# Bringing the second q chunk early, one context step further forward, in a fused attention and FFN kernel

## The chip, the cores and the metric

The program runs on one core of a Trainium2 chip. The runs were spread over several chips, and every experiment had the kernel before timed beside it on its own chip. The metric is device time of one execution in microseconds (us), as the median of several runs.

PE is the matmul engine, DVE the vector engine, ACT the scalar engine; SP issues the DMA transfers told here. PSUM is the memory that matmuls write to.

## The reference

Layer norm of x (2048 x 640), then 32 heads of attention over the last 512 keys (head size 192), a SwiGLU feed-forward net on the same normed input, and out = x + attention * silu(ffn):

```python
xn = layernorm(x)
q = (xn @ wq)                              # 2048 x (32*192)
scores = q @ k[-512:].T * 192**-0.5        # per head
o = softmax(scores) @ v[-512:]
s = o @ wo
g = silu((silu(xn @ w_gate) * (xn @ w_up)) @ w_down)
return x + s * g
```

## The kernel before

Two heads make a pair (16 pairs). For each pair there are four steps, one for each block of 512 queries. A pair first runs its four *score steps*: for each of four key chunks a product (a score tile of 128 x 1024 in fp32) and an exp of it on ACT. In between stand the three q chunks of the step that follows. Then it runs its four *context steps*: P times V, the division by the row sums, a DMA transpose of the result, and, woven in, the product with wo (the *wo tiles*) for the step two earlier. Steps are numbered through: pair 0 has 0 to 3, pair 1 has 4 to 7.

PSUM holds two buffers called `sc` (scores, wo tiles, some context accumulators) and two called `mm` (q chunks, context accumulators). A buffer can be written again when the engine that reads it has finished.

```python
def q_rows(i, j, between=None):            # chunk j of step i's q
    pr, b = divmod(i, NB)
    if j == 0:
        qTs[i] = qpool.tile([P, 3, 512], bf, name="qT")
    q_ps = mm_tile()
    for c in range(NC):                    # NC = 5
        if c == NC - 1 and between:
            between()                      # drops the held wo half here
        for h, r in enumerate((lo, hi)):
            nc.tensor.matmul(...)          # 10 in all, 64 rows each
    nc.vector.reduce_sum(qTs[i][:, j, :], ...)   # DVE, frees q_ps

def scores(i, kc):
    sc = ... sc_tile()
    for j in range(3): ...                 # 6 matmuls
    nc.scalar.activation(p_t[:, :, :], sc[:, :, :], ACT.Exp, scale=scale)

def divide(i, q2, acc, alone):             # alone: steps 0 and 1, and some of the last pair
    nc.vector.reciprocal(r[:], a_v[:, :, :, Dh : Dh + 1])
    for k in range(2):
        if k == 0 and alone:
            nc.vector.tensor_tensor(O_b[...], a_k[...], r[...], ALU.mult)
            continue
        for h in range(2):
            nc.scalar.activation(O_b[...], a_k[...], ACT.Copy, scale=r[...])
    nc.sync.dma_start_transpose(out=OT_b[...], in_=O_b[...])

def woven(i):                              # a context step with wo tiles of step i-2
    (a, b), (w, x, y, z) = (pv(i, 0), pv(i, 1)), (wo_tile(i - 2, qt) for qt in range(4))
    for part in (*a[:2], drop, w[0], *b[:2], w[1], x[0], *a[2:], x[1], y[0], *b[2:], y[1], z[0]):
        part()
    held.append(z[1])                      # the last wo half waits for the next drop

# ... second half of a wo tile ends with the DVE copy of sc into sacc (pair 0)
# or the DVE add to sacc (later pairs)

EARLY = (NB + 1, 0)                        # step 5, chunk 0
for pr in range(NPAIR):
    for b in range(NB):                    # score steps
        i = pr * NB + b
        for kc in range(KC):
            if kc < 3 and i + 1 < NS and (i + 1, kc) != EARLY:
                q_rows(i + 1, kc, drop)
            scores(i, kc)
            # ...
    for b in range(NB):                    # context steps
        i = pr * NB + b
        if i < 2:
            two(pv(i, 0), pv(i, 1))        # no wo tiles yet
            if i == 1:
                q_rows(*EARLY)             # the early chunk
        elif pr < last - 1:
            woven(i)
        # ...
```

The softmax here doesn't subtract the row's maximum and nothing guards it: scores larger than these inputs give would overflow.

Of the kernel before, what the change touches and what calls it, by code (L numbers as in the profile page):

```python
# [15 lines left out]
def kernel(  # L16
# [28 lines left out]
    NB = Sq // 512  # L45
# [28 lines left out]
    def mm_tile():  # L74
        return psum.tile([P, 2, 512], f32, name="mm", tag="mm")
# [40 lines left out]
    def load_v(pr):  # L116
        for h in range(2):
            nc.sync.dma_start(
                out=V_p[:, :, h, 0:Dh],
                in_=vv[2 * pr + h, k0:Sk, :].rearrange("(p j) d -> p j d", j=KC),  # L120
            )

    def load_wo(pr):
        wo_p = pairs[pr]["wo"] = wpool.tile([P, 3, D], bf, name="wo_p")
        nc.sync.dma_start(
            out=wo_p[:], in_=wo[pr * PD : (pr + 1) * PD, :].rearrange("(j p) d -> p j d", p=P)
        )
# [4 lines left out]
    def transpose_k(pr, j):  # L132
        d = pairs[pr]
        if j == 0:
            d["KT"] = kpool.tile([P, 3, W], bf, name="KT")
            d["ssum"] = kpool.tile([P, 3], f32, name="ssum")
            d["nmean"] = kpool.tile([P, 3], f32, name="nmean")
        nc.sync.dma_start_transpose(
            out=d["KT"][:, 0:3, j * P : (j + 1) * P],
            in_=d["K"][:, j, :, :].rearrange("p h d -> p (h d)"),  # L140
        )

    def sum_k(pr, c):
        d = pairs[pr]
        nc.vector.reduce_sum(d["ssum"][:, c : c + 1], d["KT"][:, c, :], axis=AX.X)
# [6 lines left out]
    def centre_k(pr, c):  # L152
        d = pairs[pr]
        if c == 0:
            d["khat"] = kpool.tile([P, 3, W], bf, name="khat", bufs=2)
            nc.vector.tensor_scalar(d["nmean"][:], d["ssum"][:], -1.0 / W, None, op0=ALU.mult)
        s, dst, ch, src = CENTRE[c]
        nc.vector.tensor_scalar(
            d["khat"][dst, s, :], d["KT"][src, ch, :], d["nmean"][src, ch : ch + 1], None, op0=ALU.add
        )  # L160

    qTs = {}
# [257 lines left out]

    def q_rows(i, j, between=None):
        pr, b = divmod(i, NB)
        if j == 0:
            qTs[i] = qpool.tile([P, 3, 512], bf, name="qT")
        q_ps = mm_tile()
        for c in range(NC):
            if c == NC - 1 and between:
                between()
            for h, r in enumerate((lo, hi)):
                nc.tensor.matmul(  # L430
                    q_ps[:, h, :], pairs[pr]["wq"][r, c, j * P : (j + 1) * P], xnT[r, c, b * 512 : (b + 1) * 512],
                    start=(c == 0), stop=(c == NC - 1),
                )
        with nc.allow_low_precision(reason="a sum of two, rounded once, like a copy out of PSUM"):
            nc.vector.reduce_sum(  # L435
                qTs[i][:, j, :], q_ps[:, :, :].rearrange("p h n -> p n h"), axis=AX.X
            )

    def scores(i, kc):
        khat, qT, ks = pairs[i // NB]["khat"], qTs[i], slice(kc * P, (kc + 1) * P)  # L440
        sc = mm_tile() if i == NS - 1 and kc < 2 else sc_tile()
        for j in range(3):
            for h, r in enumerate((lo, hi)):
                nc.tensor.matmul(  # L444
                    sc[:, h, :], khat[r, j, ks], qT[r, j, :], start=(j == 0), stop=(j == 2)
                )
        p_t = ppool.tile([P, 2, 512], bf, name="p_t")
        nc.scalar.activation(p_t[:, :, :], sc[:, :, :], ACT.Exp, scale=scale)  # L448
        Ps.setdefault(i, {})[kc] = p_t

    def pv(i, q2):

        pr, b = divmod(i, NB)
        st = {}

        def part(p):
            if p == 0:
                if q2 == 0:
                    Obs[i] = opool.tile([P, 4, 2, Dh], bf, name="O_b")
                    tag = "OT_l" if late(i) and pr < last else "OT_b"  # L460
                    OTs[i] = otpool.tile([P, 12, P], bf, name=tag, tag=tag, bufs=2 if tag == "OT_l" else 3)
                st["alone"] = i < 2 or (pr == last and 2 * b + q2 < 5)
                st["acc"] = sc_tile() if st["alone"] and q2 and b < 2 else mm_tile()
            acc = st["acc"]
            turn, h = divmod(p, 2)
            for kc in range(KC):
                for n, r in enumerate((lo, hi)):
                    k = n ^ turn
                    qt = 2 * q2 + k
                    m = nc.tensor.matmul(  # L470
                        acc[:, k, h * 256 : h * 256 + Dh + 1],
                        Ps[i][kc][r, h, qt * P : (qt + 1) * P], V_p[r, kc, h, 0 : Dh + 1],
                        start=(p == 0 and kc == 0), stop=(turn == 1 and kc == KC - 1),
                        skip_group_check=True,
                    )
                    after(m, st)
            if p == 1:
                turned(m, st)
            if p == 3:
                divide(i, q2, acc, st["alone"])  # L480

        return [lambda p=p: part(p) for p in range(4)]
# [46 lines left out]
    def load_xr(t):  # L529
        xrs[t] = finp.tile([P, D], bf, name="x_r", bufs=8)  # L530
        nc.sync.dma_start(out=xrs[t][:], in_=x2[t * P : (t + 1) * P, :])
# [66 lines left out]
    def wo_full(i, qt):  # L598
        pr, b = divmod(i, NB)
        t = 4 * b + qt  # L600
        sc = sc_tile()
        for n in range(2):
            wo_mm(sc[:, n, 0:HD], i, qt, n)
        s_t = sacc[:, t, :].rearrange("p (n d) -> p n d", n=2)
        if pr == 0:
            nc.vector.tensor_copy(out=s_t, in_=sc[:, :, 0:HD])
        else:
            nc.vector.tensor_tensor(s_t, s_t, sc[:, :, 0:HD], ALU.add)

        if pr == last - 1 or late(i + NB):  # L610
            nc.gpsimd.tensor_tensor(sacc[:, t, :], sacc[:, t, :], g2[:, t, :], ALU.mult)
            if pr < last - 1:
                add_x(t)

    def add_x(t):
        nc.gpsimd.tensor_tensor(sacc[:, t, :], sacc[:, t, :], xrs[t][:], ALU.add)
# [32 lines left out]
            nc.sync.dma_start(out=out2[t * P : (t + 1) * P, :], in_=ob[:])  # L649

    held = []
    EARLY = (NB + 1, 0)

    def two(x, y):
        for part in (*x[:2], *y[:2], *x[2:], *y[2:]):
            part()
# [5 lines left out]
    def woven(i):  # L662
# [5 lines that stand above are left out]
        held.append(z[1])  # L668

    for pr in range(NPAIR):  # L670
        for b in range(NB):
# [5 lines that stand above are left out]
                if pr < last:  # L677
                    if b == 0:
                        transpose_k(pr + 1, kc)
                    elif b == 2 and kc < 3:  # L680
                        sum_k(pr + 1, kc)
                    elif b == 3:
                        centre_k(pr + 1, kc)
                        if kc == 3:
                            centre_k(pr + 1, 4)
            if b == 0:
                load_v(pr)
                if pr >= last - 1:
                    for t in range(8):
                        load_xr(t + 8 if pr < last else t)  # L690
                        if pr == last:
                            add_x(t)
        if pr == last:
            break
        for b in range(NB):
            i = pr * NB + b
            if i < 2:
                two(pv(i, 0), pv(i, 1))
                if i == 1:
                    q_rows(*EARLY)  # L700
            elif pr < last - 1:
                woven(i)
            else:
                for q2 in range(2):
                    pv_full(i, q2)
                    wo_full(i - 2, 2 * q2)
                    wo_full(i - 2, 2 * q2 + 1)
            if b == 0 and pr + 2 < NPAIR:
                load_k(pr + 2)
            elif b == 1 and pr + 2 < NPAIR:  # L710
                load_wq(pr + 2)
            elif b == 2:
                load_wo(pr + 1)
    i = last * NB
# [43 lines left out]
```

## Time and profile before

| | before |
|---|---|
| time | 925.96 us (925.85 to 926.03, 3 runs) |
| span of the profiled run | 924.2 us |
| PE, DVE, ACT busy | 99%, 62%, 51% |
| recorded waits of PE from 168 to 888 us | one, 0.5 us |

How to read it: PE is the bound, so only its stops count. The recorded idle time of PE runs from the modelled end of a matmul to the next start, so it understates a stop; the starts of successive groups, compared with the same group where nothing waits, give its full length.

### The profile page before, as it was taken

How to read it: one execution, taken by the hardware profiler on the slowest of the kernel's cores; microseconds unless marked ns; L12 is line 12 of the kernel's file. 1: busy time of each engine (PE TensorE's matmuls, PEld its weight loads, DVE VectorE, ACT ScalarE, POOL GpSimd, SP SyncE). 2: the span in 40 equal slices, each digit the busy share in tenths (PEclk: the TensorE clock that was granted, in tenths of full speed). 3: DMA queues.
4: the chain of work that ended last, by engine and by line, in shares of the span. 5: the costliest groups of instructions: out<-in, count | busy, mean ns of one | idle time of the engine just before them, and what ended most of it. 6: DMA issues, size and time to landing. Idle time of an engine off the chain costs nothing.

```text
span 924.2 us, 25783 instructions
## 1 busy us (share of the span) xinstructions
PE 916.6 (99%) x11101; PEld 622.6 (67%) x11101; DVE 576.1 (62%) x844; ACT 473.8 (51%) x847; POOL 100.1 (11%) x387
## 2 busy tenths in 40 slices
PE   9999999999999999999999999999999999999997
PEld 5455555575858585868686767676767777776665
DVE  6433331467676767676666667676767676767655
ACT  4222223546464656555556465655555555656561
POOL 0000000000000000000000000000000000002977
PEclk9999999999999999999999999999999999999999
DMA  9321510044544443444636252635371717162624
GB/s 297 74 54 35 114 35 1 1 81 86 83 83 80 86 80 86 72 94 66 100 59 107 57 109 53 112 50 116 45 121 40 126 37 129 35 132 74 145 47 140
DMA packets 243810, 77.18 MB, mean 84 GB/s; under 512 B 224624, under 2 KB 243696, under 8 KB 243696
## 3 DMA queue, kind: packets, MB, share of 16 engines
q1 hardware_dynamic: 242640, 74.72, 40.7%
q8 instruction: 87, 1.43, 0.7%
q10 hardware_dynamic: 1056, 0.82, 0.3%
q14 instruction: 27, 0.22, 0.1%
HBM read 39.45 MB, written 2.62 MB: 46 GB/s over the span
## 4 chain that ended last, share of the span: by engine, by line
PE 98%; DMA 1%; DVE 1%; ACTq 0%; issue 0%; ACT 0%; DVEq 0%
PE mm L430 22%; PE sc L565 19%; PE sc L444 18%; PE mm L470 16%; PE sc L276 11%; PE mm L298 6%; PE sc L539 3%; PE mm L522 2%; PE mm L539 1%; DMA wu_sb<-in_B_w_up_dram 1%; PE mm L276 0%; PE mm L311 0%; PE sc L522 0%; PE sc L470 0%; PE mm L444 0%
## 5 line engine op out<-in xcount | busy, mean ns | idle before, releaser
L448 ACT ACTIVATE p_t<-sc 128x1024 bf16<-128x1024 f32 x254 | 253.0, 1022 | 128.9 <-PE sc L444 128.9
L435 DVE TENSOR_REDUCE qT<-mm 128x512 bf16<-128x1024 f32 x189 | 230.9, 1223 | 91.6 <-PE mm L430 89.2
L500 ACT ACTIVATE O_b<-mm,r 128x192 bf16<-128x192 f32 x486 | 164.6, 421 | 183.6 <-issue 162.4
L430 PE MATMUL mm<-xnT,wq_p 64*128 64x512 bf16 x1890 | 240.0, 376 | 0.0
L590 DVE TENSOR_TENSOR sacc<-sacc,sc 128x640 f32<-128x640 f32 x200 | 164.2, 821 | 89.5 <-PE sc L565 89.5
L565 PE MATMUL sc<-wo_p,OT_b 64*128 64x320 bf16 x2592 | 217.0, 296 | 0.0
L444 PE MATMUL sc<-qT,khat 64*128 64x512 bf16 x1524 | 198.1, 376 | 0.5 <-DVE sacc L588 0.5
L470 PE MATMUL mm<-V_p,p_t 64*128 64x193 bf16 x3520 | 186.2, 242 | 0.1
L470 PEld LDWEIGHTS <-p_t 64*128 64x128 bf16 x3584 | 162.4, 93 | 12.9 <-issue 0.6
L430 PEld LDWEIGHTS <-wq_p 64*128 64x128 bf16 x1890 | 104.7, 94 | 95.7 <-issue 0.5
L565 PEld LDWEIGHTS <-OT_b 64*128 64x128 bf16 x2592 | 139.4, 94 | 22.2
L444 PEld LDWEIGHTS <-khat 64*128 64x128 bf16 x1536 | 85.1, 94 | 80.1 <-issue 0.7
L553 POOL MEMSET turn_t<- 128x1 f32 x328 | 32.2, 98 | 697.0 <-PE mm L470 474.6
L284 DVE TENSOR_TENSOR hT<-sc,sg 128x512 bf16<-128x512 f32 x46 | 31.7, 690 | 85.2 <-ACT sg L283 85.1
L283 ACT ACTIVATE sg<-sc 128x512 bf16<-128x512 f32 x46 | 27.3, 596 | 72.4 <-PE sc L276 72.4
L276 PE MATMUL sc<-xnT,wu_sb 128*128 128x512 bf16 (+1 forms) x260 | 59.1, 354 | 0.2 <-DMA wu_sb<-in_B_w_up_dram 0.2
L276 PE MATMUL sc<-xnT,wg_sb 128*128 128x512 bf16 (+1 forms) x260 | 59.2, 354 | 0.1
L298 PE MATMUL mm<-wd_sb,hT 128*128 128x320 bf16 x384 | 56.6, 299 | 0.0
L489 DVE RECIPROCAL r<-mm 128x4 f32<-128x4 f32 x124 | 22.7, 183 | 47.8 <-PE mm L470 36.3
L298 PEld LDWEIGHTS <-hT 128*128 128x128 bf16 x384 | 37.6, 98 | 18.9
L276 PEld LDWEIGHTS <-wu_sb 128*128 128x128 bf16 x285 | 26.3, 98 | 27.2 <-DMA wu_sb<-in_B_w_up_dram 0.4
L276 PEld LDWEIGHTS <-wg_sb 128*128 128x128 bf16 x285 | 26.4, 98 | 23.1 <-issue 0.2
(68 smaller groups left out, 372.9 us busy)
## 6 DMA issues: line engine op xcount, KB each, us to landing
wo_p<-in_A_wo_dram SPq DMA_DIRECT2D x16, 480.0 KB, 4.2
K_p<-in_A_k_cache_dram SPq DMA_DIRECT2D x32, 192.0 KB, 3.3
V_p<-in_A_v_cache_dram SPq DMA_DIRECT2D x32, 192.0 KB, 3.1
wq_p<-in_A_wq_dram SPq DMA_DIRECT2D x64, 80.0 KB, 3.2
wq_p<-in_A_wq_dram SPq DMA_DIRECT2D x16, 160.0 KB, 3.4
x_r<-in_A_x_dram SPq DMA_DIRECT2D x16, 160.0 KB, 3.9
x_t<-in_A_x_dram SPq DMA_DIRECT2D x14, 160.0 KB, 3.0
OT_b<-O_b SPq DMA_TRANSPOSE x124, 2.8
```

Source lines behind the costliest of these rows:

```text
L276: nc.tensor.matmul(out, w_sb[:, c, f * P : (f + 1) * P], xnT[:, c, qc], start=(c == 0), stop=(c == NC - 1),)
L298: nc.tensor.matmul(dn[:, 0:HD], hTs[b][:, f, ti * P : (ti + 1) * P], wd_sb[:, f, cols], start=(f == 0), stop=(f == NF - 1),)
L430: nc.tensor.matmul(q_ps[:, h, :], pairs[pr]["wq"][r, c, j * P : (j + 1) * P], xnT[r, c, b * 512 : (b + 1) * 512], start=(c == 0), stop=(c ...
L435: nc.vector.reduce_sum(qTs[i][:, j, :], q_ps[:, :, :].rearrange("p h n -> p n h"), axis=AX.X)
L444: nc.tensor.matmul(sc[:, h, :], khat[r, j, ks], qT[r, j, :], start=(j == 0), stop=(j == 2))
L448: nc.scalar.activation(p_t[:, :, :], sc[:, :, :], ACT.Exp, scale=scale)
L470: m = nc.tensor.matmul(acc[:, k, h * 256 : h * 256 + Dh + 1], Ps[i][kc][r, h, qt * P : (qt + 1) * P], V_p[r, kc, h, 0 : Dh + 1], start=(p ...
L500: nc.scalar.activation(O_b[:, qt, h, :], a_k[:, h, 0:Dh], ACT.Copy, scale=r[:, k, h, :])
L539: nc.tensor.matmul(ps, OTs[i][:, 3 * qt + j, :], pairs[i // NB]["wo"][:, j, n * HD : (n + 1) * HD], start=(first and j == 0), stop=(end an ...
L553: st["turn"] = nc.gpsimd.memset(turn_t[:], 0.0)
L565: m = nc.tensor.matmul(ps[:, n, 0:HD], OTs[i][r, 3 * qt + j, :], pairs[i // NB]["wo"][r, j, n * HD : (n + 1) * HD], start=(turn == 0 and j ...
L590: nc.vector.tensor_tensor(s_t, s_t, sc[:, :, 0:HD], ALU.add)
```

## The change

In steps 0 and 1 there is no wo tile to put between, so one q chunk of a later step stands there as filler. The change takes another chunk (the second of step 5, not the first) and puts it one context step sooner. The intent is that step 4 again begins with a whole q chunk ahead of its first scores, as in the other pairs, and that the filler's own reduce is long done when its buffer is needed.

```diff
     def q_rows(i, j, between=None):
-        if j == 0:
+        if i not in qTs:
             qTs[i] = qpool.tile([P, 3, 512], bf, name="qT")
@@
-    EARLY = (NB + 1, 0)
+    EARLY = (NB + 1, 1)
@@
                 two(pv(i, 0), pv(i, 1))
-                if i == 1:
+                if i == 0:
                     q_rows(*EARLY)
```

## The prediction

> **What bounds the kernel now.** I read the page's parts 1 and 2 first, to see whether one engine carries the whole span, then the list of waits, to see whether that engine ever stops in the part that the change touches, and last the timelines of PE, DVE and ACT from 190 to 216 us, to get each margin in hundredths of a microsecond.
>
> ```profile
> PE 916.6 (99%) x11101; PEld 622.6 (67%) x11101; DVE 576.1 (62%) x844; ACT 473.8 (51%) x847; POOL 100.1 (11%) x387
> PEclk9999999999999999999999999999999999999999
> ```
>
> PE is busy 99% of 924.2 us at full granted clock. So every microsecond that PE stops is a microsecond of the end, and nothing else counts. The list of waits for PE between 168 and 214 us has one line, and from 214 to 888 us it is empty:
>
> ```profile
> PE sc L444 <- DVE sacc L588: 0.5, 1, 0.5
> ```
>
> So the most that the page itself offers is this wait. The PE timeline shows where it lies: at the seam between the context steps of pair 0 and the score steps of pair 1.
>
> ```profile
> 196.93 1.24 PE L430 MATMUL mm<-xnT,wq_p 64*128 64x512 bf16 x10
> 198.12 0.84 PE L470 MATMUL mm<-V_p,p_t 64*128 64x193 bf16 x16
> 198.79 0.58 PE L565 MATMUL sc<-wo_p,OT_b 64*128 64x320 bf16 x6
> 199.49 0.84 PE L470 MATMUL mm<-V_p,p_t 64*128 64x193 bf16 x16
> ...
> 209.06 0.99 PE L565 MATMUL sc<-wo_p,OT_b 64*128 64x320 bf16 x12
> 210.56 0.82 PE L444 MATMUL sc<-qT,khat 64*128 64x512 bf16 x6 [0.51 <-DVE sacc L588]
> 211.20 1.04 PE L430 MATMUL mm<-xnT,wq_p 64*128 64x512 bf16 x8
> 212.06 0.59 PE L565 MATMUL sc<-wo_p,OT_b 64*128 64x320 bf16 x6
> 212.47 0.40 PE L430 MATMUL mm<-xnT,wq_p 64*128 64x512 bf16 x2
> 212.69 0.83 PE L444 MATMUL sc<-qT,khat 64*128 64x512 bf16 x6
> 213.34 1.26 PE L430 MATMUL mm<-xnT,wq_p 64*128 64x512 bf16 x10
> ```
>
> The first line is the early q chunk (chunk 0 of step 5). Because it was brought early, the first scores of step 4 come straight after the wo half at 209.06, with nothing between. They need the score buffer of the wo tile before, which DVE still copies out. The next pair's seam is the undisturbed form, with a whole q chunk ahead of the scores and no wait:
>
> ```profile
> 255.69 0.99 PE L565 MATMUL sc<-wo_p,OT_b 64*128 64x320 bf16 x12
> 256.50 1.04 PE L430 MATMUL mm<-xnT,wq_p 64*128 64x512 bf16 x8
> 257.37 0.59 PE L565 MATMUL sc<-wo_p,OT_b 64*128 64x320 bf16 x6
> 257.77 0.40 PE L430 MATMUL mm<-xnT,wq_p 64*128 64x512 bf16 x2
> 257.99 0.83 PE L444 MATMUL sc<-qT,khat 64*128 64x512 bf16 x6
> ```
>
> Starts are the better clock. Twelve wo matmuls take 255.69 to 256.50, or 0.81, so at the first seam PE was free at 209.06 + 0.82 = 209.88, and the scores began at 210.56: the stop is 0.68 us, not 0.51. The same reading finds a second stop that the list of waits hides: six wo matmuls take 0.41 (257.37 to 257.77), yet after 198.79 the next line begins at 199.49, 0.70 later. So 0.29 us are lost there. The DVE and ACT timelines name both releasers:
>
> ```profile
> 198.22 1.22 DVE L435 TENSOR_REDUCE qT<-mm 128x512 bf16<-128x1024 f32 x1 [0.29 <-PE mm L430]
> ...
> 209.68 0.82 DVE L588 COPY sacc<-sc 128x640 f32<-128x640 f32 x1 [0.23 <-PE sc L565]
> ```
>
> ```profile
> 194.67 0.73 ACT L500 ACTIVATE O_b<-mm,r 128x192 bf16<-128x192 f32 x2 [1.58 <-DVE r L489]
> ...
> 197.34 0.73 ACT L500 ACTIVATE O_b<-mm,r 128x192 bf16<-128x192 f32 x2 [1.26 <-DVE r L489]
> ```
>
> The reduce of the early chunk ends at 199.44 and PE goes on at 199.49; the copy ends at 210.50 and PE goes on at 210.56. A release therefore takes about 0.05 us. A third, smaller stop: the early q chunk needs 1.075 us of issue (ten matmuls, 211.20 to 212.06 for eight), so PE could go on at 198.00, but went on at 198.12, just after the ACT work of 197.34 ended (198.07).
>
> **What the Trainium skill says.** "Perfetto Trace Analysis", section "Tensor Engine Instruction (MATMUL, LD_WEIGHTS)", says that a matmul's end is estimated and only its start observed. The trace agrees: consecutive groups overlap by about 0.17 us, and 0.51 recorded is 0.68 by starts. "TensorE: Matmul & The Clock Gate", section "The mechanism" in Part 3, says that matmuls keep program order while weight loads may be pulled ahead. So one blocked matmul holds all behind it, and a chunk helps only if it stands before the blocked one in the program. "TensorEngine Tiling (Array Packing)", section "Key Properties", says that a change of tiling mode drains the array. Every PE group from 168 to 216 us is 64*128, so moving a chunk among them adds no change of mode. "Perfetto Trace Analysis", section "Matmuls", asks that groups rotate over PSUM banks so that evacuation overlaps the next group; here two score and two mm buffers rotate, and the stops above are where that rotation is too short.
>
> **The change, part by part.** Nothing is added or removed. PE has the same 22,204 rows in both programs, ACT, POOL and SP keep their order, and DVE moves one reduce. Two parts:
>
> 1. The early chunk moves from after context step 1 to after step 0, so it runs at 194.26 instead of 196.93. It is followed by step 1, whose first accumulator takes the buffer that ACT frees at 194.67 + 0.73 = 195.40. PE could go on at 194.26 + 1.075 = 195.335 and goes on at about 195.45: the third stop stays as it was, 0.12. Step 1 then ends at 198.12 as before, and the context of step 2 starts at 198.12 as before. Its second accumulator no longer waits for the reduce (which now ends near 196.8) but for step 1's division. Step 1's accumulator ends 1.19 later than before, so its ACT work ends at 198.07 + 1.19 = 199.26, and PE is released at 199.31. It could have gone at 199.20. Before it went at 199.49, so this saves 0.18, not 0.29.
>
> 2. The chunk that is early is the second. The first stands again at its place, with the held wo half in it. From 209.88 - 0.18 = 209.70: eight q matmuls to 210.56, the wo half to 210.97, the last two q to 211.19, first scores at 211.19. The copy they need ended at 210.32, so the stop of 0.68 is gone. But now the second scores follow at once, with no chunk between. They would go at 211.19 + 0.65 = 211.84, and in the built program they wait for DVE (before, for ACT): they take the buffer of the held wo half. Its copy starts 0.62 after that half's start (257.37 and 257.99 in the next pair), so at 211.19, ends at 212.01, and releases at 212.07. A new stop of 0.23. The third q chunk starts at 212.07 + 0.65 = 212.72, against 213.34.
>
> Sum: -0.18 (reduce) -0.68 (copy) +0.23 (new stop) = -0.63; by the end points, 213.34 - 212.72 = 0.62. After that the programs are the same and PE never waits until 888 us, so the shift reaches the end whole: 925.96 - 0.62 = 925.34 us.
>
> Margins that I checked for a further stop. Exp of the first scores starts near 212.05 and ends near 213.08; the third scores need its buffer at 212.72 + 1.07 = 213.79. The second exp ends near 214.1 and the fourth scores come at 214.44. The reduce of the third chunk ends near 215.2, and step 5 needs its q near 216.2. The transposes of step 1's output are issued after the K loads, at 199.49 before; their operands are now ready at 199.26 and 199.94, the second issued near 201.2, so they keep their time. All hold, the closest by 0.2 us.
>
> **The rivals.** (a) The wait is only moved. If the copy of the held half came later, or the second scores also had to wait for an exp, the new stop would eat the gain: about 925.9. For it: two score steps stand back to back beside an exp of 1.02 us. Against it: back-to-back scores stand in every step (those x12 lines) without a wait. (b) The whole gain, 0.29 + 0.68 = 0.97, giving 924.99: it needs both replacement waits to be nothing. Against it: the copy lasts 0.82 and only 0.65 of scores covers most of it. (c) A loss. The later division of step 1 could delay the transposes, and the wo halves of step 3 would stop for a DMA. The profile gives a median of 2.8 us to landing, so the first lands by about 203 and the use is near 204.8. If it failed, up to 1 us: 926 to 926.4. (d) Nothing at all, because the chip varies: the three runs of before span 0.18 us, less than a third of the expected gain.
>
> **Range and chances.** The largest possible gain by the trace is about 1.1 us (0.68 + 0.29 + 0.12) and the plausible loss some tenths, both far from 2% (18.5 us). The centre is 925.34; rivals (a) and (b) lie about half a microsecond to each side, and chip to chip I allow 0.2. So 924.9 to 925.8. Faster by over 2%: 0.01; within 2%: 0.98; slower: 0.01.
>
> **What would show it.** The wait of 0.5 under the first scores of step 4 is gone. The first new chunk runs from about 194.26; the second accumulator of step 2 starts at about 199.31; first scores near 211.19 after eight q, six wo and two q matmuls; second scores near 212.07, 0.88 after the first instead of 0.65, with a small recorded idle (some 0.05) put down to the copy; third chunk near 212.72. I am wrong if the second scores start at 211.84 (rival b), if a wait for ACT or DMA shows up, or if the shift at 214 us is not the shift at the end.

## The result and the profile after

| | before | after |
|---|---|---|
| time, median | 925.85 us (925.52 to 926.03, 5 runs) | 925.04 us (924.93 to 925.59, 5 runs) |
| ratio | | 0.9993, 95% interval 0.9979 to 1.0006 |
| span of the profiled run | 924.2 us | 923.7 us |
| PE busy in it | 916.6 us (99%) | 917.0 us (99%) |

The three runs of the table before are the first three of these five. The ratio is the mean time of one kernel's runs over that of the other's in the same rounds, so it is not quite the ratio of the two medians. The verdict is "same": 0.8 us by the medians, 0.6 us by the ratio, and an interval that includes 1. This timing alone would not settle such a change; the trace does.

The list of waits for PE after the change, whole:

```profile
PE sc L219 <- DVE zero_t L173: 1.2, 1, 1.2
PE sc L276 <- DMA wu_sb<-in_B_w_up_dram: 0.5, 1, 0.5
PE mm L539 <- DVE s_f L640: 0.2, 1, 0.2
```

The 0.5 before the scores (L444) is gone. What is left lies at the very start and the very end of the kernel. The timeline of PE after the change (start, duration, line, operation, output and inputs, count):

```profile
194.44 1.24 PE L430 MATMUL mm<-xnT,wq_p 64*128 64x512 bf16 x10
195.63 0.84 PE L470 MATMUL mm<-V_p,p_t 64*128 64x193 bf16 x16
...
198.97 0.58 PE L565 MATMUL sc<-wo_p,OT_b 64*128 64x320 bf16 x6
199.50 0.84 PE L470 MATMUL mm<-V_p,p_t 64*128 64x193 bf16 x16
...
209.87 1.04 PE L430 MATMUL mm<-xnT,wq_p 64*128 64x512 bf16 x8
210.74 0.59 PE L565 MATMUL sc<-wo_p,OT_b 64*128 64x320 bf16 x6
211.14 0.40 PE L430 MATMUL mm<-xnT,wq_p 64*128 64x512 bf16 x2
211.36 1.70 PE L444 MATMUL sc<-qT,khat 64*128 64x512 bf16 x12
212.88 1.26 PE L430 MATMUL mm<-xnT,wq_p 64*128 64x512 bf16 x10
```

This run reached the first context matmul at 191.77, before it was 191.59, so 0.18 is to be taken from every time here when it is held against the prediction. The reader is to see three things. The second accumulator of step 2 follows the wo half ahead of it by 0.53 (198.97 to 199.50), where it was 0.70 in the kernel before; the reduce that it waited for then now ends at 196.95. The first scores come at once after the chunk (211.14 to 211.36). And twelve score matmuls take 1.52 to the next chunk (211.36 to 212.88), where twelve without a stop take 1.30: the new stop of 0.22 that the wait list doesn't show.

Three lines of other engines belong to these places: the reduce of the early chunk, which no longer stops PE, the ACT division of step 1's accumulator, which releases PE at the first place, and the DVE copy of the held wo half, which releases it at the last:

```profile
195.72 1.23 DVE L435 TENSOR_REDUCE qT<-mm 128x512 bf16<-128x1024 f32 x1 [0.29 <-PE mm L430]
```

```profile
198.72 0.73 ACT L500 ACTIVATE O_b<-mm,r 128x192 bf16<-128x192 f32 x2 [2.46 <-DVE r L489]
```

```profile
211.36 0.82 DVE L588 COPY sacc<-sc 128x640 f32<-128x640 f32 x1 [0.85 <-PE sc L565]
```

The division ends at 199.45 and PE goes on at 199.50. The copy ends at 212.18, and the second scores started at 212.88 - 0.65 = 212.23. (Asked for the window 212.22 to 212.40 alone, the trace gives 212.24, which is 0.88 after the first scores.)

### The profile page after: what moved, and what is told of

Same layout as the page of the kernel before. It is cut to its first block, busy times and chain, and to the rows that moved or that the text cites. A ratio compares the mean times of both kernels' runs of the same rounds, so it can differ in the third digit from the quotient of the medians.

```text
span 923.7 us, 25785 instructions
## 1 busy us (share of the span) xinstructions
PE 917.0 (99%) x11101; PEld 626.2 (68%) x11101; DVE 576.2 (62%) x844; ACT 473.7 (51%) x847; POOL 100.1 (11%) x387
## 3 DMA queue, kind: packets, MB, share of 16 engines
q8 instruction: 87, 1.43, 0.7%
## 4 chain that ended last, share of the span: by engine, by line
PE 98%; DMA 1%; DVE 0%; ACTq 0%; issue 0%; DVEq 0%
PE mm L430 22%; PE sc L565 19%; PE sc L444 18%; PE mm L470 16%; PE sc L276 11%; PE mm L298 6%; PE sc L539 3%; PE mm L522 2%; PE mm L539 1%; DMA wu_sb<-in_B_w_up_dram 1%; PE mm L276 0%; PE mm L311 0%; PE sc L522 0%; PE sc L470 0%; PE mm L444 0%
## 5 line engine op out<-in xcount | busy, mean ns | idle before, releaser
L444 PE MATMUL sc<-qT,khat 64*128 64x512 bf16 x1524 | 198.4, 377 | 0.1
L444 PEld LDWEIGHTS <-khat 64*128 64x128 bf16 x1536 | 85.9, 94 | 79.0 <-issue 0.4
L298 PE MATMUL mm<-wd_sb,hT 128*128 128x320 bf16 x384 | 56.6, 300 | 0.0
L298 PEld LDWEIGHTS <-hT 128*128 128x128 bf16 x384 | 37.5, 98 | 18.9
```

Of the source, the lines that this page charges most:

```text
L298: nc.tensor.matmul(dn[:, 0:HD], hTs[b][:, f, ti * P : (ti + 1) * P], wd_sb[:, f, cols], start=(f == 0), stop=(f == NF - 1),)
L444: nc.tensor.matmul(sc[:, h, :], khat[r, j, ks], qT[r, j, :], start=(j == 0), stop=(j == 2))
```

## The experiments

Two measures serve all of them. The **seam** is the time by starts from the first context matmul of pair 0 to the first q chunk of step 6: the stretch in which the two programs differ. The **rest** is from there to the start of the last three wo matmuls of the kernel. A seam without any stop should last 24.12 (before) - 0.68 - 0.29 - 0.12 = 23.03 us.

| kernel | seam starts | seam | rest | time, median (lowest to highest) | before, same chip |
|---|---|---|---|---|---|
| before | 191.59 | 24.12 | 703.17 | 925.85 | |
| after | 191.77 | 23.49 | 703.19 | 925.04 (924.93 to 925.59) | 925.85 |
| after, again | 191.40 | 23.48 | 703.20 | 925.17 (925.14 to 925.34) | 925.82 |
| after, third time | 191.48 | 23.49 | 703.19 | 925.25 (925.07 to 925.47) | 926.00 |
| second chunk, late place | 192.55 | 23.66 | 703.17 | 925.36 (925.07 to 926.44) | 925.82 |
| first chunk, early place | 191.79 | 23.95 | 703.19 | 925.74 (925.45 to 926.38) | 925.82 |
| no chunk early | 191.29 | 24.14 | 703.16 | 925.48 (925.36 to 925.66) | 925.82 |
| third chunk, early place | 191.37 | 23.90 | 703.19 | 925.59 (925.55 to 926.02) | 926.10 |
| wo half sooner | 191.38 | 23.28 | 703.17 | 924.96 (924.73 to 925.93) | 926.10 |
| DVE divides | 191.57 | 23.24 | 703.20 | 925.36 (924.86 to 925.44) | 926.10 |
| both mends | 191.95 | 23.03 | 703.20 | 925.17 (924.79 to 925.62) | 926.10 |
| both mends, again | 191.12 | 23.03 | 703.20 | 924.58 (924.50 to 924.65) | 926.00 |

The rest is the same to 0.04 us in all twelve profiles, so nothing that happens in the seam is given back or multiplied later. The start of the seam varies by 1.43 us between profiles. This scatter arises in the first 40 us of the program: the first product of the down projection (L298) starts between 38.92 and 40.35 us, and from there to the seam it is 152.19 to 152.20 us in all twelve. From the last three wo matmuls to the end of the span it is 5.25 to 5.34 us. So in the profiles the times differ by the first 40 us and by the seam, and by nothing else above 0.1 us. One source of the scatter is in the lists of waits: in the "second chunk, late place" run, which started its seam last, PE stood 1.2 us for the first gate weights, and in the first "both mends" run it stood 0.5 us for the up weights. The runs that were only timed have no trace; that their scatter has the same source is likely, but not shown.

### The changed kernel again

No edit. It also served as the yardstick on the same chip as the next three.

> The changed kernel once more, as the yardstick for the runs beside it. The seam is counted by starts on PE, from the first context matmul of pair 0 to the first q chunk of step 6; it was 215.71 - 191.59 = 24.12 us before and 215.26 - 191.77 = 23.49 after. Theory (three named stops, each with its releaser): 23.49 again, with stops of 0.12 (third stop, ACT division), 0.10 (second accumulator of step 2, ACT division) and 0.23 (second scores of step 4, copy of the held wo half). Rival (the 0.63 is chance of one run): a seam that differs by over 0.05. Timed: 0.4 to 0.8 us under before.

Measured: seam 23.48, and 23.49 in a third profile.

> The changed kernel a third time, beside the version with both mends on one chip. Theory: seam 23.49; timed 0.4 to 0.8 us under before.

The seam is reproducible to 0.01 us; the medians lie 0.65 and 0.75 under before on the same chips. The 0.63 of the first profile was no chance.

### Only the choice of the chunk

```diff
-    EARLY = (NB + 1, 0)
+    EARLY = (NB + 1, 1)
@@     (and "if i not in qTs"; the place stays i == 1)
```

> Only the choice of the chunk changes: the second chunk is early, but still after context step 1. Theory (the two parts add up): the stop of 0.68 before the first scores of step 4 is gone and 0.23 comes before the second scores, while the second accumulator of step 2 still waits 0.29 for the reduce: seam 24.12 - 0.45 = 23.67, second accumulator 0.70 after the wo half that precedes it. Rival (the place of the chunk makes the gain): 24.12. Timed: about 0.45 us under before, if the end follows.

Measured: seam 23.66. The timeline of this kernel:

```profile
199.75 0.58 PE L565 MATMUL sc<-wo_p,OT_b 64*128 64x320 bf16 x6
200.45 0.84 PE L470 MATMUL mm<-V_p,p_t 64*128 64x193 bf16 x16
...
212.31 1.70 PE L444 MATMUL sc<-qT,khat 64*128 64x512 bf16 x12
213.84 1.26 PE L430 MATMUL mm<-xnT,wq_p 64*128 64x512 bf16 x10
```

The 0.70 from wo half to accumulator is there as before, and the two scores take 1.53. So the choice of the chunk is worth 0.46 of the 0.63 and brings the new stop with it.

### Only the place

```diff
-                if i == 1:
+                if i == 0:
                     q_rows(*EARLY)
@@     (EARLY stays (NB + 1, 0))
```

> Only the place changes: the first chunk is early, after context step 0. Theory: the stop at the second accumulator of step 2 falls from 0.29 to 0.10 or 0.12, the stop of 0.68 before the first scores of step 4 stays: seam 24.12 - 0.18 = 23.94. Rival (the place alone makes the gain, the copy wait dissolves because everything before it is sooner): 23.5. Timed: about 0.2 us under before, inside the spread.

Measured: seam 23.95. The stop in front of the scores is untouched:

```profile
209.08 0.99 PE L565 MATMUL sc<-wo_p,OT_b 64*128 64x320 bf16 x12
210.58 0.82 PE L444 MATMUL sc<-qT,khat 64*128 64x512 bf16 x6 [0.51 <-DVE sacc L588]
```

The place is worth 0.17. The two parts add up: 0.46 + 0.17 = 0.63. The rival held that the copy's wait would dissolve once everything before it is sooner. It doesn't, because the copy moves along with the wo tile that it reads. By the timer this part is lost in the scatter (925.74 against 925.82).

### No early chunk at all

```diff
-    EARLY = (NB + 1, 1)
+    EARLY = None
@@
-                if i == 0:
-                    q_rows(*EARLY)
```

> No chunk is early: all three of step 5 stand in step 4, as in the other pairs. The same matmuls in all. Theory: the stops before the scores of step 4 (0.68, 0.23) are both gone, since a whole chunk stands ahead of each, and so is the third stop; but the context steps of step 2 come 1.2 us sooner, and its first wo half has to wait for the transpose of step 0's output (issued at 195.4, 2.8 us at least to landing): a stop of 0.6 to 1.0 put down to DMA or shown as a late weight load. Seam 23.03 + 0.6 to 1.0 = 23.6 to 24.1. Rival (an early chunk is of no use any more): seam 23.0 to 23.1, and about 1.0 us faster than before.

Measured: seam 24.14, at the upper edge and a little beyond. There were two stops, not one. The timeline:

```profile
196.63 0.83 PE L470 MATMUL mm<-V_p,p_t 64*128 64x193 bf16 x16
197.98 0.58 PE L565 MATMUL sc<-wo_p,OT_b 64*128 64x320 bf16 x6 [0.51 <-DMA OT_b<-O_b]
...
203.51 0.57 PE L565 MATMUL sc<-wo_p,OT_b 64*128 64x320 bf16 x6
204.33 0.58 PE L565 MATMUL sc<-wo_p,OT_b 64*128 64x320 bf16 x6 [0.25 <-DMA OT_b<-O_b]
```

By starts they are 197.98 - 196.63 - 0.67 = 0.68 and 204.33 - 203.51 - 0.41 = 0.41, together 1.09, and 23.03 + 1.09 = 24.12. The first is the transpose of step 0's output, as expected. The second, which was not expected, is that of step 1's output: the transpose issued at 199.20 in this run, after the two K loads, took 5.1 us to landing, where those of step 0 took 2.8. So the filler is needed, and what it covers is a DMA: taking it away costs all that the change gained. The second stop is not a fixed cost: this transpose took 3.3 to 5.1 us to landing in the twelve profiles, and with the 3.6 of the kernel before it would have landed at 202.8 here, before its use at 203.92 (203.51 + 0.41). (The median, 925.48, is 0.34 under before although the seam is no shorter; this profile started its seam 0.30 sooner than that of before, and its spread of 0.30 is narrow. What made five starts in a row early is not known.)

### The third chunk instead

```diff
-    EARLY = (NB + 1, 1)
+    EARLY = (NB + 1, 2)
```

> The third chunk is early instead, after context step 0. Theory (what matters is what then stands back to back, and a score tile lives until its exp has read it): the first two scores each have a chunk ahead, so both copy waits are gone (0.68 and 0.23), but the second, third and fourth scores of step 4 follow one another, 0.65 of PE against 1.02 of exp each, so the fourth waits for the second's exp by about 0.63. Stops 0.12 + 0.10 + 0.63: seam 23.03 + 0.85 = 23.88. Rival (only the wo copy can stop the scores): 23.25, which would beat the change.

Measured: seam 23.90. Both copy waits are gone, and the scores stop for an exp:

```profile
212.69 1.47 PE L444 MATMUL sc<-qT,khat 64*128 64x512 bf16 x12
214.63 0.82 PE L444 MATMUL sc<-qT,khat 64*128 64x512 bf16 x6 [0.46 <-ACT p_t L448]
```

1.94 from start to start less 1.30 is 0.64, against 0.63 expected (recorded: 0.46). The ACT timeline shows why:

```profile
213.55 2.96 ACT L448 ACTIVATE p_t<-sc 128x1024 bf16<-128x1024 f32 x3 [0.70 <-PE sc L444]
```

The exp of the second scores starts at 213.55, lasts 1.02 to 214.57, and the fourth scores, which take its buffer, start at 214.63. Here three score tiles in a row outrun ACT with two buffers; two in a row don't. Of the three chunks at this place the second gives the shortest seam (23.49 against 23.95 and 23.90).

### The held wo half sooner

The new stop of 0.22 was put down to the copy of the held wo half. Here that half is dropped two matmuls sooner, in step 4 alone:

```diff
-            if c == NC - 1 and between:
+            if c == NC - (2 if i == NB + 1 else 1) and between:
```

> The changed kernel, but in step 4 alone the held wo half is dropped two matmuls sooner (before the fourth of five parts of the q chunk, not before the fifth). Theory: the copy then begins 0.215 sooner against the second scores, so their stop of 0.23 falls to 0.02 or less: seam 23.49 - 0.22 = 23.27, and twelve score matmuls from their start to the third chunk take 1.30, not 1.52. Rival (the 0.23 is exp or a cost of two score steps in a row after wo): no change, 23.49.

Measured: seam 23.28.

```profile
209.49 0.83 PE L430 MATMUL mm<-xnT,wq_p 64*128 64x512 bf16 x6
210.14 0.59 PE L565 MATMUL sc<-wo_p,OT_b 64*128 64x320 bf16 x6
210.55 0.61 PE L430 MATMUL mm<-xnT,wq_p 64*128 64x512 bf16 x4
210.98 1.49 PE L444 MATMUL sc<-qT,khat 64*128 64x512 bf16 x12
212.29 1.26 PE L430 MATMUL mm<-xnT,wq_p 64*128 64x512 bf16 x10
```

```profile
210.76 0.82 DVE L588 COPY sacc<-sc 128x640 f32<-128x640 f32 x1 [0.64 <-PE sc L565]
```

The twelve scores take 1.31. The copy now begins 0.22 before the scores (210.76 and 210.98), not together with them, and the stop is gone (0.01 at most). So the stop was the copy, not exp and not a cost of scores after wo.

### DVE divides alone

```diff
+        if i < 2: nc.vector.tensor_tensor(O_b[:, 2 * q2 : 2 * q2 + 2, :, :], a_v[:, :, :, 0:Dh], r[:].to_broadcast([P, 2, 2, Dh]), ALU.mult)
-        for k in range(2):
+        for k in range(2) if i >= 2 else ():
@@     (two lines below are joined into one, so that line numbers stay)
```

> The changed kernel, but in steps 0 and 1 of pair 0 DVE divides both halves in one instruction (768 elements a partition, estimated 0.96 us from 0.56 for 384 and 0.18 for 4) instead of one half each on DVE and then ACT (0.56 + 0.10 + 0.73). Theory: the accumulator is released 0.4 us sooner, so the stop of 0.12 after the early chunk and the stop of 0.10 before the second accumulator of step 2 are gone: seam 23.49 - 0.22 = 23.27. Rival (the 0.12 is what a passage from q to context matmuls costs): 23.49 or 23.39.

Measured: seam 23.24. One timeline of PE and one of DVE:

```profile
194.24 1.24 PE L430 MATMUL mm<-xnT,wq_p 64*128 64x512 bf16 x10
195.32 0.83 PE L470 MATMUL mm<-V_p,p_t 64*128 64x193 bf16 x16
```

```profile
193.99 0.96 DVE L490 TENSOR_TENSOR O_b<-mm,r 128x768 bf16<-128x768 f32 x1
```

The chunk now takes 1.08 to the next start, not 1.19, so a passage from q to context matmuls costs nothing of itself and the 0.12 was the division. The wo half to the second accumulator takes 0.40 (198.66 to 199.06), so that stop is gone too. The one instruction on 768 elements took 0.96, as estimated (a straight line through the two figures that the estimate names gives 0.94). It wins because the two pieces on two engines had been run one after the other: 0.56 on DVE, 0.10 between, 0.73 on ACT.

### Both mends together

Both edits above in one kernel; the second time beside the changed kernel on one chip.

> Both of the two edits above together. Theory (the stops are independent): seam 23.05, no stop left, 1.07 us less than before and 0.44 less than the change; timed about 0.9 to 1.1 us under before. Rival (one stop only hides behind another): seam 23.27.

> The version with both mends once more, beside the changed kernel on one chip. Theory: seam 23.03, 0.45 us shorter than the changed kernel, and the stretch after the seam the same to 0.04 us; timed 0.3 to 0.6 us under the changed kernel, if the scatter of the start (the seam began between 191.29 and 192.55 us in nine profiles) does not hide it. Rival (the stretch after the seam gives the gain back): the stretch longer by 0.3 or more and no difference in the times.

Measured: seam 23.03 in both profiles, which is the sum without any stop. The stops are independent, and of those named none is left in the seam. The first timing (925.17) is 0.93 under before on its chip, as expected, but shows no lead over the changed kernel (925.04 and 925.17); that profile began its seam late, at 191.95. On one chip with the changed kernel the second timing gave 924.58 (924.50 to 924.65) against 925.25 (925.07 to 925.47): ranges that do not meet, and a ratio to before of 0.9985, interval 0.9971 to 0.9998. The difference of 0.67 is a little over the 0.3 to 0.6 expected. The seam accounts for 0.46 of it; in the two profiles the start of the seam differs as well, 191.12 against 191.48. By its seam this version beats both kernels, twice, by 0.46 and 1.09. By the timer it stands apart from before in the second only (0.15%); the interval of the first, 0.9978 to 1.0003, includes 1.

## Why the prediction was right

- **The bound.** What the seam gains reaches the end whole: the rest after the seam is 703.16 to 703.20 us in all profiles.
- **Stops by starts, not by recorded idle.** 0.68, 0.29 and 0.12 were read where the page records 0.51 and nothing. The seam without stops came out at 23.03, just before's 24.12 less these three.
- **Place of the chunk, -0.18.** Measured alone 0.17. The accumulator went on at 199.50 - 0.18 = 199.32, predicted 199.31.
- **Copy wait gone, -0.68, and new stop, +0.23.** Measured together alone -0.46, predicted -0.45; the new stop 0.22. First scores at 211.36 - 0.18 = 211.18 (211.19), third chunk at 212.70 (212.72).
- **Third stop unchanged, 0.12.** The step from chunk to context stayed 1.19 until DVE divided alone.
- **A sign that was not seen.** The prediction expected a small recorded idle (some 0.05) put down to the copy at the second scores. They did start 0.88 after the first, but the list of waits has no entry for them: this stop can be read from starts alone.
- **Sum.** Seam -0.63 against -0.62 predicted; time 925.04 against 925.34. That last difference is not mechanism: the median lies 0.81 under before while the seam is 0.63 shorter, and the repeats gave 0.65 and 0.75. The variable start before the seam is enough to explain it, but which part of it did so in the first five runs was not measured.
- **The range is a weak test.** 924.9 to 925.8 holds the medians of kernels whose seam is shorter by 0.17 (925.74) and by nothing (925.48). That the time fell inside says little about the mechanism; the starts in the trace say it.
- **Margins that were read wrongly.** For the transposes of step 1 the prediction took 2.8 us to landing, the median of the whole kernel, had the first down by about 203, and said that they keep their time. The kernel before had 3.6 for this very one. In the profile after, it was issued when predicted (199.68 - 0.18 = 199.50) but took 4.8 us and so landed at 204.5, and was needed at 205.02 (204.61 plus six wo matmuls, 0.41). The margin was 0.5, not nearly 2. It held in all three profiles of the change, and that was in part luck: with no early chunk it didn't. And "the closest by 0.2 us" does not come out of the prediction's own numbers: the closest that it works out is 214.44 - 214.1 = 0.34. Measured, the second exp ended at 214.16 and the fourth scores came at 214.61 (213.96 + 0.65), a margin of 0.45.
- **A count.** The 22,204 rows of PE stand in no page: both pages show 11,101 matmuls and 11,101 weight loads, 22,202 in all. That the two programs are equal in this holds. The prediction's remark on a change of tiling mode is tested by no run, since none changes the mode here.
- **The rivals.** (b), the whole 0.97, fails because both replacement waits are real. Only the two mends take them away; with the third stop they bring the seam to 0.63 + 0.46 = 1.09 under before. (a) and (c) did not occur, but both have a place where they do: with the third chunk the wait moves to an exp, and with no chunk it moves to a DMA. (d), nothing to be seen, is what a single timing gives, since each interval of the ratio includes 1. But the median of the change was lower in all three, by 0.81, 0.65 and 0.75, in two of them with ranges that do not meet (925.34 against 925.56, 925.47 against 925.61), and the seam decides it.

## What to carry to other kernels

Where one engine is full, look for its stops by comparing the starts of equal groups of instructions; the recorded idle left out some 0.17 us of each stop here, and short stops whole. Filler work between two stages is worth what it covers at the place from which it came as well as at the place to which it goes: take it from where its absence leaves two tiles in a row that the reading engine can still keep up with, and put it far enough ahead that its own buffer is free again when needed. A sum of named stops predicts tenths of a microsecond that the timer cannot resolve, if each has its releaser and its replacement worked out.

## What the Trainium skill lacked or had wrong

- "Perfetto Trace Analysis", section "Tensor Engine Instruction (MATMUL, LD_WEIGHTS)", says that a matmul's end is estimated, but not what this does to idle time. Here recorded idle was 0.16 to 0.18 us short of each stop (0.51 for 0.68, 0.25 for 0.41, 0.46 for 0.64), and stops of 0.29, 0.22 and 0.12 had no entry in the list of waits.
- The same page, section "DVE / Act Engine Instruction (TENSOR_ADD, Activation, etc)", names the propagation of a semaphore after the recorded end but gives no duration there. Here PE started 0.05 to 0.06 us after the end of the DVE or ACT instruction that released it (210.50 to 210.56, 199.45 to 199.50, 214.57 to 214.63).
- "Perfetto Trace Analysis", section "Matmuls", asks for rotation over PSUM banks. It doesn't say how many tiles in a row a rotation of two can bear. Here two score tiles in a row (0.65 us each against 1.02 of exp) ran without an exp stop, and the third in a row stopped 0.64.
- None of the places used here says how far the landing of one small DMA transpose can move. Here the same transpose (the first of step 1's output, issued right after two K loads of 192 KB each) took 3.3 to 5.1 us to landing in the twelve profiles, against a median of 2.8 for all 124 transposes of this kind in the kernel. In the profiles of before, after and no chunk early the second of the K loads took 3.5, 4.2 and 4.6 where the transpose took 3.6, 4.8 and 5.1. That the loads delay it is likely, but no run tests it.
